# Retention attention by pairs of units, grouped by the tiling of TensorE

## The chip, the cores and the metric

One core of a Trainium2 chip runs the whole program. The metric is the device time in microseconds. Engines: TensorE (PE) multiplies, VectorE (DVE), ScalarE (ACT) and GpSimd (POOL) do the rest, SyncE (SP) issues all DMAs on one queue.

## The reference, cut to what matters

```python
def _attn_ref(q, k, v):                       # B=4, H=8, S=576, D=64
    scores = (1/sqrt(D)) * q @ k.T
    gamma = 1 - 2.0 ** (-5 - arange(H))
    Dmat = where(i >= j, gamma_h ** (i - j), 0)
    return (scores * Dmat) @ v
def _moe_ref(x, w_in, g_ln, w_sg, b_sg, w_out):
    h = gelu(x @ w_in); u, v = h[..., :512], h[..., 512:]
    v_n = (v - mean) / sqrt(var + 1e-6) * g_ln
    v_s = einsum('ts,bsd->btd', w_sg, v_n) + b_sg[None, :, None]
    return x + (u * v_s) @ w_out
def _moe2_ref(x, g_ln, w_ch1, w_ch2):
    return x + relu(layernorm(x) * g_ln @ w_ch1) @ w_ch2
out = _moe2_ref(_moe_ref(_attn_ref(q, k, v)))
```

## The kernel before

The program is written out in order by hand: each engine executes its instructions in the order of the code, and nothing is moved later. PSUM has 8 banks in a ring; one of them, `b_75`, belongs to the decoding of weights.

**Attention.** A unit n is one batch and one pair of heads: 16 units, 128 partitions for two heads of 64. A sequence is four chunks of 128 positions and a rest of 64. The decay of the reference is split into a factor of the row (i), a factor of the column (j) and a state carried from chunk to chunk. For a unit: `load_unit` fetches q, k, v (1120 KB in one DMA, five buffers); `prep_unit` scales k on ACT; `scores` (L246) multiplies q and k, and a mask is applied as PSUM is read (L256; on DVE, each fourth on ACT and POOL); `states` (L282) sums k times v by chunk and a scan (L290, DVE) carries them on; `attend_near` (L315) adds masked scores times v, `attend` (L327, L346) the carried state times q. `scores` of the rest (L269) and `attend_rest` (L303) run once in two units. DVE multiplies the result by the factors of the rows and writes it to `xb` (L333, L350). PE is used in tiles here: 64x128 (L246), 64x64 (L303, L327, L346, L269) and 128x64 (L282, L315). The masks (`form_masks`, L499; `form_rest`, L507) are formed from a table during the warm-up products (L530), the rows by four products with K=8 (`form_rows`, L515).

**Gated MLP.** For each batch b: v tiles (`v_tile`, 5 or 4), u chunks (`u_chunk`, 4), spatial gate (`sg_chunk` L706, 4), `w_out_tile`. Each float32 operand is a high and a low part and each product three products (`mm3`, L137 to L139). The low part of the normalized v (`vnl`, L645) and of weights (`split`, L361) is subtracted on POOL. In `sg_chunk` DVE multiplies the gate into u (L724, L727), ACT casts the high part `glh` (L735), and POOL or DVE subtracts `gll` (L738).

**Third part.** In the last batch, the features of `moe2` are scaled (L939), mixed on POOL (L953) and split (`split_features`, L960 on ACT and L961 on DVE).

**The decoding of weights.** w_in, w_out and w_ch come as words of float64. A piece is four steps on DVE (L156, L160, L163, L165) with one square on ACT (L162); after it the weight is split, or stored by DMA. `w_sg` is float32 and only split (ACT L360, L394, and POOL). `background(n)` does the next n steps. How many steps stand where is written in two tables: `UNIT`, two digits for each unit of attention, and `PACE`, for each b the digits of v tiles, u chunks, sg chunks and w_out tiles. What is left is drained after the u chunks of b=3, ahead of `split_features`:

```python
        if last:
            for _ in bg:
                pass
            free(f64_at[2])
...
            feat = split_features(0)
            next(feat)
```

Of the kernel before, what the change touches and what calls it, by code (L numbers as in the profile page):

```python
# [21 lines left out]
NP = H // 2  # L22
# [21 lines left out]
    ("13446", "3140", "2211", "01021"),  # L44
# [3 lines left out]
UNIT = "00 00 21 22 31 11 10 12 21 13 22 11 32 20 01 32".split()  # L48
# [26 lines left out]
O_MASKR = 16  # L75
O_HEAD = O_MASKR + NP * R
O_GROW = O_HEAD + C
TA = O_GROW + NP * C
TS = (NP + 1) * C
# [8 lines left out]
def const_tables():  # L88
    g = np.array(GAMMA, np.float64)
    p = np.arange(128)  # L90
    tab = np.zeros((128, TF + TS), np.float64)
    tab[:, O_TRI:O_TRI + C] = np.arange(C)[None, :] >= p[:, None]
    tab[:, O_GP:O_GP + H] = g[None, :] ** -p[:, None]
    tab[:, O_GK:O_GK + H] = g[None, :] ** (C - p[:, None])
    for hp in range(NP):
        gp = g[2 * hp + p // D][:, None]
        tab[:, O_GC + hp * NC:O_GC + (hp + 1) * NC] = gp ** C * (np.arange(NC)[None, :] > 0)
        tab[:, O_GR + hp:O_GR + hp + 1] = gp ** -(p % R)[:, None]
        tab[0:H, TF + (hp + 1) * C:TF + (hp + 2) * C] = np.arange(H)[:, None] == 2 * hp + p[None, :] // D
    tab[0:H, TF:TF + C] = g[:, None] ** np.arange(C)[None, :] / np.sqrt(D)  # L100
    return tab.astype(np.float32)
# [3 lines left out]
def kernel(  # L105
# [7 lines left out]
    tab_in: bass.AP,  # L113
    params: bass.AP,
# [74 lines left out]
    ld = es_a.enter_context(tc.tile_pool(name="ld", bufs=5))  # L189
# [8 lines left out]
    first = pa.tile([128, D * NC], F32, tag="y", bufs=3, name="first")  # L198

    def load_tab(part):  # L200
        if part == 0:
            nc.sync.dma_start(out=first[:, 0:TF], in_=tab_in[:, 0:TF])
        else:
            nc.sync.dma_start(out=tab[0:H, O_HEAD:], in_=tab_in[0:H, TF:])

    NU = B * NP
    units = {}
# [3 lines left out]
    def load_unit(n):  # L211
        t = ld.tile([128, AW], F32, tag="ld", name="ld")
        if n == 0:

            to, src = (z[:, 0:2 * S].rearrange("p (a s) -> p a s", a=2) for z in (t, attn[n]))
            for x, y in ((0, 2 * C), (2 * C, S)):
                nc.sync.dma_start(out=to[:, :, x:y], in_=src[:, :, x:y])
                if x == 0:
                    load_tab(0)
            nc.sync.dma_start(out=t[:, 2 * S:], in_=attn[n, :, 2 * S:])  # L220
        else:
            nc.sync.dma_start(out=t, in_=attn[n])
        units[n] = dict(ld=t)

    def prep_unit(n):
        u = units[n]
        hp = n % NP
        t = u["ld"]
        u["qT"] = t[:, 0:S]
        u["kT"] = t[:, S:2 * S]  # L230
        u["k"] = t[:, 2 * S:2 * S + NC * C].rearrange("p (c e) -> p c e", c=NC)
        o = 2 * S + NC * C
        v = t[:, o:]
        u["v"] = v
        for h in range(2):
            k = u["k"][:, :, h * D:(h + 1) * D]
            act.activation(out=k, in_=k, func=ACTF.Copy, scale=col(tab, 2 * hp + h))

    def scores(n):
        u = units[n]  # L240
        hp = n % NP
        p = u["p"] = pa.tile([128, 2, NC, C], F32, tag="p", name="p")
        sc = [bank() for h in range(2)]
        for c in range(NC):
            for h in range(2):
                pe.matmul(  # L246
                    sc[h][:, c * C:(c + 1) * C], u["kT"][h * D:(h + 1) * D, c * C:(c + 1) * C],
                    u["qT"][h * D:(h + 1) * D, c * C:(c + 1) * C], start=True, stop=True,
                )
        for h in range(2):  # L250
            x = sc[h].rearrange("p (c i) -> p c i", c=NC)
            on = dve
            if h and n % 2:
                act.copy(p[:, h], x)
                x, on = p[:, h], pool
            on.tensor_tensor(  # L256
                out=p[:, h], in0=x, in1=mask[:, 2 * hp + h].unsqueeze(1).to_broadcast([128, NC, C]), op=ALU.mult,
            )
            free(sc[h])
        if n % 2 == 0:  # L260
            return

        rest = u["rest"] = bank()
        pr = u["pr"] = pa.tile([128, 2 * R], F32, tag="pr", name="pr")
        for x in range(2):
            w = units[n - 1 + x]
            for h in range(2):
                r = slice(h * D, (h + 1) * D)
                pe.matmul(  # L269
                    rest[r, x * R:(x + 1) * R], w["kT"][r, NC * C:], w["qT"][r, NC * C:], start=True, stop=True,  # L270
                    skip_group_check=True,
                )
        dve.tensor_tensor(out=pr, in0=rest[:, 0:2 * R], in1=col(tab, O_MASKR + (hp - 1) * R, 2 * R), op=ALU.mult)

    def states(n):
        u = units[n]
        us = bank()
        us_c = us[:, 0:NC * D].rearrange("p (e c) -> p c e", c=NC)
        for c in range(NC):
            for h in range(2):  # L280
                r = slice(h * D, (h + 1) * D)
                pe.matmul(  # L282
                    us_c[r, c], u["k"][:, c, r],
                    u["v"][:, c * C + h * D:c * C + (h + 1) * D], start=True, stop=True,
                )


        y = pa.tile([128, D * NC], F32, tag="y", bufs=3, name="y")
        u["y"] = y.rearrange("p (e c) -> p c e", c=NC)
        dve.tensor_tensor_scan(  # L290
            out=y, data0=decay[:, n % NP], data1=us[:, 0:NC * D], initial=0.0, op0=ALU.mult, op1=ALU.add
        )
        free(us)

    def attend_rest(n):
        if n % 2 == 0:
            return
        u = units[n]
        for x in range(2):
            o = u["rest"][:, (2 + x) * R:(3 + x) * R]  # L300
            for h in range(2):
                r = slice(h * D, (h + 1) * D)
                pe.matmul(  # L303
                    o[r], units[n - 1 + x]["v"][r, NC * C:], u["pr"][r, x * R:(x + 1) * R], start=x == 0, stop=False,
                    skip_group_check=True,
                )

    def attend_near(n):
# [1185 lines left out]
```

## Time and profile before

| what | value |
|---|---|
| median of 3 runs | 662.07 us (661.23 to 662.87) |
| the profiled execution | 661.1 us |
| span in the trace | 659.3 us |
| granted TensorE clock, mean | 1.000 |
| PE, busy share of the span | 99% |
| DVE, ACT, POOL | 70%, 47%, 46% |

The span runs from the first to the last instruction that the profiler recorded; the execution's own time is 1.8 us longer. All times of the trace are microseconds from the span's start. A timeline row is: start, duration, engine, line, operation, out<-in with shapes, number of instructions joined in the row, and in brackets an idle time ahead of it and what ended it. The durations of joined PE rows overlap, so a rate is read from start to start. Attention runs to 78.4 us, the gated MLP to about 285, and the third part to the end.

### The profile page before, as it was taken

The numbers are of one execution on the slowest core, as the hardware profiler recorded it, in microseconds if no ns is written. First come the engines' busy times: TensorE is split into PE (matmuls) and PEld (weight loads), VectorE is DVE, ScalarE is ACT, GpSimd is POOL, SyncE is SP. The second block draws the span as 40 slices with busy tenths as digits, with TensorE's granted clock in tenths as the row PEclk, the third lists the DMA queues.
The fourth block names the chain that finished last, engine by engine and source line by source line (L and its number), as shares of the span: only waits on it lengthen the run. The fifth ranks groups of instructions, "written<-read, shape, count | busy, mean of one in ns | idle before, by whom it ended". The sixth has DMA issues, their size and how long they took to land.

```text
span 659.3 us, 12482 instructions
## 1 busy us (share of the span) xinstructions
PE 652.3 (99%) x4428; PEld 592.9 (90%) x4428; DVE 458.7 (70%) x925; ACT 310.7 (47%) x638; POOL 306.0 (46%) x290
## 2 busy tenths in 40 slices
PE   8999999999999999999999999999999999999997
PEld 6888899899889989998898889988898889999996
DVE  5799769789799885877888643555543345458894
ACT  4454595275277457524454533233535313335443
POOL 0354658225325617955555694265558742410000
PEclk9999999999999999999999999999999999999999
DMA  8999638677687685579996868799999689999734
GB/s 317 365 371 352 192 106 231 228 243 231 225 296 230 194 244 135 173 276 398 310 309 245 266 209 269 241 369 371 341 354 373 200 299 342 363 364 413 263 129 160
DMA packets 97230, 181.23 MB, mean 275 GB/s; under 512 B 9608, under 2 KB 47112, under 8 KB 93456
## 3 DMA queue, kind: packets, MB, share of 16 engines
q1 hardware_dynamic: 97168, 180.44, 80.7%
q8 instruction: 35, 0.57, 0.3%
q14 instruction: 27, 0.22, 0.1%
HBM read 122.99 MB, written 56.62 MB: 272 GB/s over the span
## 4 chain that ended last, share of the span: by engine, by line
PE 92%; DVE 3%; DMA 2%; ACT 2%; POOL 1%; issue 1%; SPq 0%; DVEq 0%; POOLq 0%; ACTq 0%
PE b L139 24%; PE b L137 23%; PE b L138 23%; PE b L788 6%; PE b L1265 3%; PE b L246 2%; PE b L315 2%; PE b L327 2%; PE b L1266 2%; DMA raw<-in_w_in_dram 1%; PE b L282 1%; PE b L530 1%; PE b L722 1%; PE b L721 1%; POOL vnl L645 1%
## 5 line engine op out<-in xcount | busy, mean ns | idle before, releaser
L137 PE MATMUL b<-fe,w 128*128 128x384 f32 x336 | 113.2, 337 | 0.0
L139 PE MATMUL b<-fe,w 128*128 128x384 f32 x336 | 113.0, 336 | 0.0
L138 PE MATMUL b<-fe,w 128*128 128x384 f32 x336 | 112.7, 335 | 0.0
L139 PE MATMUL b<-w,h 128*128 128x512 f32 (+1 forms) x270 | 98.1, 363 | 0.0
L138 PE MATMUL b<-w,h 128*128 128x512 f32 (+1 forms) x270 | 97.9, 363 | 0.0
L137 PE MATMUL b<-w,h 128*128 128x512 f32 (+1 forms) x270 | 96.8, 358 | 0.0
L869 POOL TENSOR_TENSOR w<-raw_w,w 128x512 fp32r<-128x512 f32 x30 | 39.6, 1321 | 58.3 <-ACT w L868 53.2
L137 PEld LDWEIGHTS b<-fe,w 128*128 128x128 f32 x336 | 63.1, 188 | 3.8 <-DVE t L1122 0.9
L138 PEld LDWEIGHTS b<-fe,w 128*128 128x128 f32 x336 | 63.1, 188 | 2.7
L139 PEld LDWEIGHTS b<-fe,w 128*128 128x128 f32 x336 | 63.0, 188 | 0.0
L139 PEld LDWEIGHTS b<-w,h 128*128 128x128 f32 x270 | 51.0, 189 | 7.7
L137 PEld LDWEIGHTS b<-w,h 128*128 128x128 f32 x270 | 51.0, 189 | 6.0 <-issue 0.2
L138 PEld LDWEIGHTS b<-w,h 128*128 128x128 f32 x270 | 50.9, 189 | 6.1
L162 ACT ACTIVATE raw<-raw 128x512 f32<-128x512 f32 x44 | 29.9, 679 | 54.5 <-DVE b L160 47.3
L1099 ACT ACTIVATE h<-b 128x384 fp32r<-128x384 f32 x32 | 15.7, 491 | 82.7 <-DVE b L1128 54.7
L589 POOL TENSOR_TENSOR st<-st,par 128x1 f32<-128x1 f32 x36 | 22.1, 616 | 49.6 <-DVE st L588 49.5
L1100 DVE SCALAR_TENSOR_TENSOR h<-b,h 128x384 fp32r<-128x384 f32 x32 | 17.8, 556 | 30.7 <-ACT h L1099 30.7
L137 PE MATMUL b<-w_sg,vnh 128*128 128x288 f32 x128 | 37.8, 295 | 0.0
L139 PE MATMUL b<-xt_hi,w_in 128*128 128x288 f32 x128 | 37.7, 295 | 0.0
L139 PE MATMUL b<-w_sg,vnl 128*128 128x288 f32 x128 | 37.7, 295 | 0.0
L138 PE MATMUL b<-w_sg,vnh 128*128 128x288 f32 x128 | 37.7, 295 | 0.0
L138 PE MATMUL b<-xt_lo,w_in 128*128 128x288 f32 x128 | 37.7, 294 | 0.0
(196 smaller groups left out, 1695.3 us busy)
## 6 DMA issues: line engine op xcount, KB each, us to landing
w<-ws_dram SPq DMA_DIRECT2D x96, 256.0 KB, 5.0
ld<-in_attn_dram SPq DMA_DIRECT2D x15, 1120.0 KB, 8.4
raw<-in_w_ch_dram SPq DMA_DIRECT2D x32, 512.0 KB, 4.9
ws_dram<-w SPq DMA_DIRECT2D x16, 896.0 KB, 7.6
w<-wb_dram SPq DMA_DIRECT2D x14, 1024.0 KB, 7.9
w_dram<-c SPq DMA_DIRECT2D x32, 256.0 KB, 3.1
wb_dram<-fe SPq DMA_DIRECT2D x32, 256.0 KB, 5.1
raw_w<-w_dram SPq DMA_DIRECT2D x30, 256.0 KB, 4.3
```

Of the source, the lines that this page charges most:

```text
L137: pe.matmul(ps, lh, rh, start=first, stop=False, skip_group_check=True)
L138: pe.matmul(ps, lh, rl, start=False, stop=False, skip_group_check=True)
L139: pe.matmul(ps, ll, rh, start=False, stop=last, skip_group_check=True)
L162: act.activation(out=f(w1), in_=f(w1), func=ACTF.Square)
L246: pe.matmul(sc[h][:, c * C:(c + 1) * C], u["kT"][h * D:(h + 1) * D, c * C:(c + 1) * C], u["qT"][h * D:(h + 1) * D, c * C:(c + 1) * C], sta ...
L315: pe.matmul(o[r, c * C:(c + 1) * C], v[:, c * C + h * D:c * C + (h + 1) * D], p[:, h, c], start=(c == 0), stop=(c == NC - 1), skip_group_c ...
L589: pool.tensor_tensor(out=st[:, 4:5], in0=st[:, 3:4], in1=col(par, O_MH), op=ALU.pow)
L788: pe.matmul(ps, g, wo[k][:, w], start=done[0] == 1, stop=done[0] == 3 * KE, skip_group_check=True)
L869: pool.tensor_tensor(out=t[:, 1], in0=raw, in1=f(t[:, 0]), op=ALU.subtract)
L1099: act.activation(out=t[:, 0], in_=v, func=ACTF.Relu)
L1100: dve.scalar_tensor_tensor(out=t[:, 1], in0=v, scalar=0.0, in1=f(t[:, 0]), op0=ALU.max, op1=ALU.subtract)
L1265: pe.matmul(ps, e[:, 0, x], t, start=begin, stop=False, skip_group_check=True)
```

## The change

- Units go in pairs (a, b). The products of a pair stand in three groups by PE's tiling: scores of both (64x128); rest scores, the far part and the rest of the pair before (64x64); states and near part (128x64). The far part of a pair thus comes one pair later (`finish(k - 1)`).
- The factors of the rows are multiplied into q on POOL (`scale_q`) and no longer into the result; ACT copies the result to `xb` (`put`). All masks are on DVE.
- The loads are split in two: `kk` (544 KB, four buffers) and `qv` (576 KB, six buffers).
- The rows are formed by two products of 128x128 by 512 columns after the first scores; the masks are formed from their PSUM banks by DVE (L537, L546) after that, in place of the warm-up.
- `v_products(0, 0)` of the gated MLP, which ran inside the last unit, stands behind attention.
- Attention has 32 background steps, in `PAIR`, where there were 44. In b=3 the v tiles have none, and the u chunks twelve; w_in is decoded with its right half first. `w_sg` is cast in b=0.

PE, one pair of units ahead of it and behind it in the same pattern: before (a row of `L246` stands for alternating rows of two banks; `b_..` are PSUM banks, `ld` a unit's load, `p` and `pr` masked scores, `y` the carried states):

```order
L246 MATMUL b_79<-ld 128x128
...
L303 MATMUL b_78<-pr,ld 64x64 x4
L282 MATMUL b_76<-ld 64x64 x8
L315 MATMUL b_77<-p,ld 64x128 x8
L327 MATMUL b_77<-ld,y 64x128 x6
L346 MATMUL b_78<-ld,y 64x64 x4
L246 MATMUL b_80<-ld 128x128
...
L269 MATMUL b_80<-ld 64x64 x4
L282 MATMUL b_82<-ld 64x64 x8
L315 MATMUL b_76<-p,ld 64x128 x8
L327 MATMUL b_76<-ld,y 64x128 x6
```

and now (`kk` and `qv` are the two loads):

```order
L254 MATMUL b_81<-qv,kk 128x128
L254 MATMUL b_76<-qv,kk 128x128
...
L273 MATMUL b_81<-qv,kk 64x64 x4
L325 MATMUL b_82<-qv,y 64x128 x6
L325 MATMUL b_78<-qv,y 64x128 x6
L340 MATMUL b_80<-pr,qv 64x64 x4
L340 MATMUL b_80<-qv,y 64x64 x4
L294 MATMUL b_76<-qv,kk 64x64 x16
L316 MATMUL b_79<-p,qv 64x128 x8
L316 MATMUL b_77<-p,qv 64x128 x8
```

The tiling changes eight times in two units before, and three times now.

ACT behind attention, in the v tiles of b=0 (`t` is a v tile after GELU, `vnh` the high part of its normalized form), before:

```order
L619 ACT_TABLE_LOAD
L619 ACTIVATE t,st<-b_79 128x512
L619 ACTIVATE t,st<-b_82 128x512
L603 ACTIVATE st<-st 128x1
L604 ACTIVATE vnh,st<-t,st 128x512
L360 CAST w_out<-c 128x512
L162 ACTIVATE raw<-raw 128x512
```

and now:

```order
L658 ACT_TABLE_LOAD
L658 ACTIVATE t,st<-b_81 128x512
L658 ACTIVATE t,st<-b_78 128x512
L642 ACTIVATE st<-st 128x1
L643 ACTIVATE vnh,st<-t,st 128x512
L362 CAST w_in<-c 128x512
L362 CAST w_sg<-raw_sg 128x576 x2
L658 ACTIVATE t,st<-b_79 128x512
L642 ACTIVATE st<-st 128x1
L643 ACTIVATE vnh,st<-t,st 128x512
L362 CAST w_sg<-raw_sg 128x576 x2
L396 CAST w_sg<-raw_sg 128x576
```

The five casts of `w_sg` moved here out of attention, and w_out's went behind them.

DVE from the u chunks of b=3 to the first sg multiply (`x_t` is a turned tile of x, `fe` a feature part), before:

```order
L759 STREAM_TRANSPOSE x_t<-xb 128x4x4x32 x3
L961 TENSOR_TENSOR fe<-x_raw,fe 128x768
L759 STREAM_TRANSPOSE x_t<-xb 128x4x2x32
L724 SCALAR_TENSOR_TENSOR b_78<-b_78,par,b_bc 128x288
L727 TENSOR_TENSOR u<-u,b_78 128x288
```

and now, where the rows of `L154` to `L163` stand once before these, and once more ahead of the last piece:

```order
L154 TENSOR_SCALAR b_75<-raw 128x512
L158 SCALAR_TENSOR_TENSOR b_75<-raw,b_75 128x512
L161 SCALAR_TENSOR_TENSOR b_75<-raw,b_75 128x512
L163 SCALAR_TENSOR_TENSOR c<-raw,b_75 128x512
L798 STREAM_TRANSPOSE x_t<-xb 128x4x4x32 x2
...
L1000 TENSOR_TENSOR fe<-x_raw,fe 128x768
L798 STREAM_TRANSPOSE x_t<-xb 128x4x2x32
L763 SCALAR_TENSOR_TENSOR b_76<-b_76,par,b_bc 128x288
L766 TENSOR_TENSOR u<-u,b_76 128x288
```

Five pieces of four steps, three in the u chunks and two drained, now stand on DVE between the last v tile's normalization and `L1000`; before there was none.

The diff, cut to its core:

```diff
-    ("13446", "3140", "2211", "01021"),
+    ("00000", "4440", "2211", "01021"),
...
-UNIT = "00 00 21 22 31 11 10 12 21 13 22 11 32 20 01 32".split()
+PAIR = "01 12 12 22 22 22 23 34".split()
...
+    def load_kk(n):
+        if n < NU:
+            t = kk[n] = ld.tile([128, S + NC * C], F32, tag="kk", bufs=4, name="kk")
+            for x, y in ((0, S + NC * C),) if n else ((0, S), (S, S + NC * C)):
+                nc.sync.dma_start(out=t[:, x:y], in_=attn[n, :, x:y])
+                yield
...
+    def scale_q(n):
+        q = units[n]["qT"]
+        row = col(tab, O_LATE + n % NP * C, C)
+        x = q[:, 0:NC * C].rearrange("p (c i) -> p c i", c=NC)
+        pool.tensor_tensor(out=x, in0=x, in1=row.unsqueeze(1).to_broadcast([128, NC, C]), op=ALU.mult)
+        x = q[:, NC * C:]
+        pool.tensor_tensor(out=x, in0=x, in1=row[:, 0:R], op=ALU.mult)
...
+    def put(n):
+        u = units[n]
+        b, hp = divmod(n, NP)
...
+        act.copy(xb[b][:, hp, 0:NC * C], u["o"])
+        free(u["o"])
...
-        for k in range(KE):
-            t = slot("w_in").rearrange("p (a n) -> p a n", a=2)
-            wi.append(t)
-            for x in range(0, F1, 512):
+            wi.append(slot("w_in").rearrange("p (a n) -> p a n", a=2))
+        for x in (512, 0):
+            for k in range(KE):
...
+    def form_rows():
+        for x in range(2):
+            pe.matmul(each[x], one, grow[:, x * 512:(x + 1) * 512], start=True, stop=True)
...
+    def form_masks(x):
+        for h in range(x * 4, x * 4 + 4):
+            dve.scalar_tensor_tensor(
+                out=mask[:, h], in0=each[x][:, h % 4 * C:(h % 4 + 1) * C], scalar=col(first, O_GP + h),
+                in1=col(first, O_TRI, C), op0=ALU.mult, op1=ALU.mult,
+            )
...
+    def finish(k):
+        for n in (2 * k, 2 * k + 1):
+            far(n)
+            put(n)
+        attend_rest(k)
+        put_rest(k)
+
+    for k in range(NPAIR):
+        a, b = 2 * k, 2 * k + 1
+        scores(a)
+        if k == 0:
+            form_rows()
+            scale_k(a)
+            form_masks(0)
+        masks(a)
+        if k == 0:
+            form_decay()
+            form_late()
+            free(each[0])
+            states(a)
+            form_rest()
+        else:
+            scale_k(a)
+        if k == 1:
+            finish(k - 1)
+            load(load_qv(a + 4), load_qv(b + 4))
+        scores(b)
+        masks(b)
+        scale_k(b)
+        scores_rest(k)
+        mask_rest(k)
+        scale_q(a)
+        scale_q(b)
+        background(1 if k == 0 else int(PAIR[k][0]))
+        if k == 0:
+            form_masks(1)
+            free(each[1])
+        if k > 1:
+            finish(k - 1)
+            load(load_qv(a + 4), load_qv(b + 4))
+        if k:
+            states(a)
+        states(b)
+        scans(k)
+        near(a)
+        near(b)
+        load(load_kk(a + 4), load_kk(b + 4))
+        background(int(PAIR[k][1]))
...
+    finish(NPAIR - 1)
     es_a.close()
...
-            v_tile(0, 0, v_ps)
+            v_tile(0, 0)
```

## Rows read from the trace of the kernel before

**Rows 1.** The page: busy time of each engine, its share and instructions.

```profile
PE 652.3 (99%) x4428; PEld 592.9 (90%) x4428; DVE 458.7 (70%) x925; ACT 310.7 (47%) x638; POOL 306.0 (46%) x290
```

**Rows 2.** What PE waited for: engine, line, releaser: us in total, times, longest.

```profile
PE b L530 <- ACT zero L495: 2.3, 1, 2.3
PE b L315 <- POOL p L256: 0.2, 1, 0.2
```

**Rows 3.** Timeline of PE over one pair of units in attention's middle.

```profile
43.82 1.16 PE L246 MATMUL b<-ld 64*128 64x128 f32 x16
44.91 0.45 PE L269 MATMUL b<-ld 64*64 64x64 f32 x8
45.29 0.69 PE L282 MATMUL b<-ld 128*64 128x64 f32 x16
45.81 1.05 PE L315 MATMUL b<-p,ld 128*64 128x128 f32 x16
46.78 0.98 PE L327 MATMUL b<-ld,y 64*64 64x128 f32 x12
...
52.00 0.38 PE L246 MATMUL b<-ld 64*128 64x128 f32 x2
```

**Rows 4.** Timelines of PE and of DVE at the start.

```profile
8.44 1.15 PE L515 MATMUL b<-tab 8*128 8x128 f32 x8
3.82 1.66 DVE L499 TENSOR_SCALAR formed<-first 128x128 f32<-128x128 f32 x8 [2.42 <-DMA first<-in_tab_dram]
5.40 2.12 DVE L507 TENSOR_SCALAR tab<-first 64x64 f32<-64x64 f32 x8
8.54 1.29 DVE L256 TENSOR_TENSOR p<-b,formed 128x512 f32<-128x512 f32 x2 [1.02 <-PE b L246]
20.64 0.69 DVE L156 TENSOR_SCALAR b<-raw 128x512 uint32<-128x512 uint32 x1
```

**Rows 5.** Busy time in windows of 5 us; the last columns are PE's clock, DMA share, GB/s.

```profile
35.00:40.00 5.00, 5.00 (x88) 4.42 (x86) 5.00 (x11) 2.25 (x6) 1.48 (x2) 1.00 1.00 397
45.00:50.00 5.00, 5.00 (x98) 4.45 (x100) 4.93 (x10) 3.45 (x7) 3.51 (x3) 1.00 0.88 315
```

**Rows 6.** b=0: timelines of PE, ACT, POOL; PE's chain; DMA issues to 80 us.

```profile
78.45 0.50 PE L137 MATMUL b<-w_in,xt_hi 128*128 128x512 f32 x1
79.21 1.28 ACT L619 ACT_TABLE_LOAD   x1
101.43 0.62 ACT L644 CAST vnh<-t 128x512 fp32r<-128x512 f32 x1
102.72 1.31 POOL L645 TENSOR_TENSOR vnl<-t,vnh 128x512 fp32r<-128x512 f32 x1
104.08 0.40 PE b L722
raw_sg<-in_w_sg_dram SPq DMA_DIRECT2D x5, 288.0 KB, 3.2
```

**Rows 7.** b=3: timelines of DVE, ACT and PE.

```profile
242.57 0.69 DVE L156 TENSOR_SCALAR b<-raw 128x512 uint32<-128x512 uint32 x1
245.42 0.15 DVE L588 TENSOR_SCALAR st<-st 128x1 f32<-128x1 f32 x1
258.44 1.92 DVE L961 TENSOR_TENSOR fe<-x_raw,fe 128x768 fp32r<-128x768 f32 x1 [3.52 <-ACT fe L960]
260.64 0.48 DVE L724 SCALAR_TENSOR_TENSOR b<-b,par,b_bc 128x288 f32<-128x288 f32 x1
262.46 2.22 DVE L961 TENSOR_TENSOR fe<-x_raw,fe 128x768 fp32r<-128x768 f32 x1
269.68 0.95 DVE L961 TENSOR_TENSOR fe<-rows,fe 128x768 fp32r<-128x768 f32 x1
269.80 0.62 ACT L735 CAST glh<-u 128x512 fp32r<-128x512 f32 x1 [1.73 <-DVE u L727]
271.24 2.91 PE L788 MATMUL b<-w_out,glh 128*128 128x512 f32 x12
```

More of the change, by code (lines that the diff above doesn't have):

```diff
@@ L209 @@
     xt = {}
[L211 to L223, printed above, removed]
@@ new lines, in masks, with scores_rest @@
+    def masks(n):
+        u = units[n]
+        p = u["p"] = pa.tile([128, 2, NC, C], F32, tag="p", name="p")
+        for h in range(2):
+            dve.tensor_tensor(
+                out=p[:, h], in0=u["sc"][h].rearrange("p (c i) -> p c i", c=NC),
+                in1=mask[:, 2 * (n % NP) + h].unsqueeze(1).to_broadcast([128, NC, C]), op=ALU.mult,
+            )
+            free(u["sc"][h])
+    rests = {}
+    def scores_rest(k):
+        t = rests[k] = bank()
+        for x in range(2):
+            u = units[2 * k + x]
+            for r in half:
+                pe.matmul(
+                    t[r, x * R:(x + 1) * R], u["kT"][r, NC * C:], u["qT"][r, NC * C:], start=True, stop=True,
+                    skip_group_check=True,
+                )
@@ L244, in scores, with mask_rest, states @@
+    def mask_rest(k):
+        pr = units[2 * k]["pr"] = pa.tile([128, 2 * R], F32, tag="pr", name="pr")
+        dve.tensor_tensor(
+            out=pr, in0=rests[k][:, 0:2 * R], in1=col(tab, O_MASKR + 2 * k % NP * R, 2 * R), op=ALU.mult
+        )
+    sums = {}
+    def states(n):
+        k, x = divmod(n, 2)
+        if x == 0:
+            sums[k] = bank()
+        u = units[n]
+        o = sums[k][:, x * NC * D:(x + 1) * NC * D].rearrange("p (e c) -> p c e", c=NC)
         for c in range(NC):
@@ L260, in scores @@
[L260 to L292, printed above, removed]
-        free(us)
@@ L295, in attend_rest @@
[L295 to L308, printed above, removed]
+                    o[half[h], c], u["k"][:, c, half[h]], u["v"][:, c * C + h * D:c * C + (h + 1) * D],
@@ new lines, in states, with scans @@
+                    start=True, stop=True, skip_group_check=True,
+                )
+    def scans(k):
+        us = sums.pop(k)
+        for x in range(2):
+            y = pa.tile([128, D * NC], F32, tag="y", bufs=4, name="y")
+            units[2 * k + x]["y"] = y.rearrange("p (e c) -> p c e", c=NC)
+            dve.tensor_tensor_scan(
+                out=y, data0=decay[:, (2 * k + x) % NP], data1=us[:, x * NC * D:(x + 1) * NC * D], initial=0.0,
+                op0=ALU.mult, op1=ALU.add,
+            )
+        free(us)
@@ L309, in attend_near, with near @@
+    def near(n):
         u = units[n]
@@ L522 @@
-    act.copy(col(tab, 0, H), col(first, O_GK, H))
-    for hp in range(NP):
-        act.copy(
-            decay[:, hp].rearrange("p (e c) -> p e c", c=NC),
-            col(first, O_GC + hp * NC, NC).unsqueeze(1).to_broadcast([128, D, NC]),
-        )
-    warm = bank()
-    for _ in range(WARM):
-        pe.matmul(warm, zero[:, 0:128], zero, start=True, stop=True)
-    free(warm)
-    for hp in range(NP):
-        form_masks(hp)
-    form_rest()
-    prep_unit(0)
-    scores(0)
-    form_rows()
```

237 lines of the change are left out of this document (112 added, 125 removed).

## The prediction, made before the run

> **What bounds the kernel now.** I read the page first. TensorE is busy in 99% of the span, and no other engine in more than 70% [rows 1]; the list of what PE waited for holds two waits, 2.3 us for the first memset and 0.2 us in unit 1 [rows 2]. So only two things can move the time: PE work that goes away or is added, and a wait that PE gets where it has none. The timeline of PE over one pair of units then prices the work [rows 3], the timelines of the first 10 us price the start [rows 4], and those of b=0 and b=3 show how late DVE, ACT and POOL may be before PE waits [rows 6, 7]. All sums are made against the profiled execution, 661.1 us, which lies 0.97 us under the median of 662.07; I add that at the end. A measurement of this kernel can tell about 0.3%, or 2.0 us.
>
> **Attention: the switches of tiling.** Busy PE hides a cost between groups of different tile sizes. From start to start, L246 takes 1.09 (43.82 to 44.91) and L315 0.97 (45.81 to 46.78), each for 16 products of 128 columns; L246 has another tiling ahead of it and behind it, L315 only behind [rows 3]. If a switch's price s is shared by the two sides, the 0.12 is half of it: s = 0.24. The second pair has products of 64 columns: L269, eight, between two switches, takes 0.38 (44.91 to 45.29), and L282, sixteen, with one switch ahead of it, 0.52 (45.29 to 45.81). With x for eight products, x + s = 0.38 and 2x + s/2 = 0.52 give x = 0.22 and s = 0.16. I take 0.17, near the second pair, since there the switch is half of what is measured and in the first a tenth. A pair of units has 8 switches now, and 3 in the new order (64x128, then 64x64, then 128x64; first order excerpt): 5 fewer, 0.87 us a pair and 6.9 for eight; with the last unit's own switches 7.2. With the ends of attention left as they are, bounds are 5.2 at 0.13 and 9.6 at 0.24.
>
> **Attention: what is added.** The rows are formed by two products of 512 columns in place of four of 128. The L515 group takes 1.15 with the tail of its last product and a switch in it [rows 4], so 512 columns cost about 0.9; twice that in place of once is +0.9. The larger addition is at the start. DVE formed masks from 3.82, under the warm-up, eight of L499 at 0.2 and eight of L507 at 0.265 [rows 4]. Now L537 reads PSUM, so nothing is formed before the row products end, which is near 9.6 for the first (8.44 + 0.9 and the way to DVE). Ahead of near(1) DVE then has four L537 (0.9), two masks of unit 0 (1.2 by L256), form_rest (2.1 as L507) and two masks of unit 1 (1.2): 9.6 + 5.4 = 15.0 [rows 4]. PE comes to near(1) earlier. I put its waits at 2.6: 0.4 for states(1) behind ACT's scaling, 0.8 for near(1), 0.9 for a bank of pair 1's scores, whose masks stand on DVE behind the first L154, which waits for its raw weight until about 20 us (20.64 before [rows 4]), and 0.5 for pair 2's far part. Bounds: 1.0 if only the first two hold, and 4.5 if the bank's wait comes in two pairs more. In a later pair DVE has four masks, rest mask, two scans and about one decode piece, 2.4 + 0.3 + 1.2 + 2.5 = 6.4 us of a new period of 7.3: enough. ACT's put and POOL's scale_q are off PE's path by a period.
>
> The sum for attention is -7.2 + 0.9 + 2.6 = **-3.7**; its end moves from 75.5 (the first product behind it at 78.45 [rows 6], less the 2.9 of v product (0,0) that ran inside it, twelve products of 512 columns like the L788 row [rows 7]) to 71.8.
>
> **The loads.** Each unit's 1120 KB come as 544 and 576 KB. At a pair period of 7.3 us, two units and one 512 KB weight piece are 2.8 MB, 385 GB/s. The window from 35 to 40 us gives 397 GB/s, and that from 45 to 50, with its engines 88% busy, 315 [rows 5], so it is just enough. The first of these has 512 KB weight pieces among the 1120 KB loads and was full all the same, so I charge the smaller loads nothing and keep the poor window as a rival. The Trainium skill ("DMA: Bandwidth & Descriptors", the table of measured bandwidth) speaks against the split: it asks for at least 1 MiB in a transfer for three quarters of the peak. By it the halves would run slower, and the sum would be that of rival 3; by the row it stays.
>
> **b=0: most of the gain is not handed on.** Attention now has 32 background steps in place of 44; w_sg's five pieces are cast by ACT in b=0's v tiles (second order excerpt). Before, ACT runs from the table load at 79.21 to the last cast of vnh, 101.43 + 0.62 = 102.05; POOL then needs vnl, 102.72 + 1.31 = 104.03, and PE's L722 starts at 104.08 [rows 6], with no slack at all. Afterwards the table load waits for v product (0,0), 71.8 + 2.9 = 74.7. ACT's work up to the last cast is about the same (five w_sg casts in place of three w_out casts and three squares), but the third and fourth w_sg casts want raw buffers that come free only after POOL's subtraction (1.31, as vnl) and a load (3.2): 4.5 less some 2 us of other ACT work leaves 2.6 of waiting [rows 6]. So the last cast ends at 74.7 + 22.84 + 2.6 = 100.1, and POOL's w_out subtraction and vnl bring L722 to about 102.5. PE would be there at 104.08 - 3.7 = 100.4: it waits 2.1, and **-1.5** is handed on. Bounds: 0 (the casts wait once more) and -3.7 (ACT has room in other places).
>
> **b=3: a new wait.** The three pieces not decoded in attention push all later ones back; b=3 keeps five, three in its u chunks and two drained behind them (third order excerpt). A piece takes DVE 242.57 to 245.42, 2.85 us [rows 7], about 2.95 with its neighbours. All five stand on DVE ahead of the feature split L1000 and of the first sg multiply. Before, DVE had 3.5 us of idle time there, and L961 started at 258.44 only because ACT's fe was late; the first multiply was at 260.64 [rows 7]. Now DVE starts the first piece when the last normalization is through, near 247.4; five pieces are 14.75, four turns of x 2.6, the st group 0.75, and 1.6 is lost where a square on ACT stands behind GELU and the scaling of features: 267.0 for L1000 and 268.1 for the first multiply, 7.5 later. From there DVE makes up about 1 us, since L1000 runs beside an idle POOL (0.95 as at 269.68, not 1.92 or 2.22 [rows 7]). ACT's cast of glh for m=2 starts not at 269.80 but at 276.3 and ends at 276.9. PE's w_out tile starts at 271.24 and needs it four products later, 271.24 + 4 x 0.23 = 272.15 [rows 7]. PE waits **4.7 us**; bounds 3.0 (two more us made up) and 6.5 (the square waits twice). No wait would come if the first multiply were at 262.4 or earlier. PE has no idle time behind it in which this could be made up [rows 2].
>
> **The sum.** -1.5 + 4.7 = +3.2: 664.3 against 661.1, and 665.3 against the median; I round to **665.0**.
>
> **The rivals.**
> 1. *DVE's queue in b=3 is short enough* (chance 0.27). For it: DVE's 3.5 us idle there, and ACT starts earlier because v tiles of b=3 lose five squares (its five decode pieces). Against it: 14.75 us of decode does not fit between 247.4 and 262.4 beside 3.3 of turns and st. If it fits up to 1 us, the time is 662.07 - 1.5 to -3.7 + 0 to 1, 658.4 to 661.5: faster.
> 2. *The wait and the full gain* (0.15): ACT in b=0 keeps up, -3.7 + 4.7 = +1.0, or -3.7 + 3 = -0.7: 661.4 to 663.1, no change that could be told.
> 3. *The loads decide attention* (0.08). At 315 GB/s [rows 5] 2.8 MB take 8.9 us, no less than the old period of 8.18 (43.82 to 52.00, [rows 3]); it decides from a period of 7.3, 385 GB/s. Attention then gains nothing, so b=0 hands on nothing: 662.07 + 4.7 = 666.8, up to 670.
> 4. *A switch costs nothing* (0.03): the difference between L246 and L315 is then the tile, and only +0.9, +2.6 and +4.7 are left, about 669.
>
> **How the numbers follow.** The forecast itself has 0.47, and its own range by the bounds is 662.6 to 667.5. Below 660.1 lies rival 1 with most of its chance: faster 0.24. Within 2.0 us of 662.07 lie the rest of rival 1, rival 2 and the low end of the forecast: 0.23. Slower 0.53. The range 658.8 to 667.8 takes in the forecast and all but the best end of rival 1, and leaves out the loads and the costless switch.
>
> **What would show it.** Right: pairs of about 7.3 us on PE; the first v product behind attention near 71.8; a wait of PE for POOL's vnl of some 2 us at sg chunk 0 of b=0; in b=3 five pieces back to back on DVE, the first L763 near 266.6 (268.1 less the 1.5), and a wait of PE of 4 to 5 us at the first w_out tile for glh. Wrong: no wait at that tile; a wait of PE for a load in the pairs; a period of 8 us; an end of attention near 75.

## The result and the profile after

| | before | after |
|---|---|---|
| median | 662.47 us (661.23 to 664.12, 4 runs) | 672.29 us (669.72 to 673.35, 4 runs) |
| ratio of after to before | | 1.0141 [1.0104, 1.0178] |
| profiled execution, its span | 661.1, 659.3 us | 669.72, 667.8 us |
| mean granted clock | 1.000 | 0.995 |

The change makes the kernel slower by 1.4%, where 665.0 was forecast: attention became 1.9 us shorter, and two later stages became 11.0 longer. The profiled execution is the quickest of the four; the other three had clocks of 0.986 to 0.992.

Line numbers have moved: far part L325, near part L316, w_out tile L827, sg multiply L763 and L766, glh L774, gll L777, vnl L684. The page, to be held against [rows 1]:

```profile
PE 650.6 (97%) x4424; PEld 593.2 (89%) x4424; DVE 454.5 (68%) x912; ACT 317.6 (48%) x657; POOL 319.4 (48%) x314
PEclk9999998999999999899999999999999999999999
```

PE's busy time fell by 1.7 us and the span rose by 8.5. What PE waited for stood in two rows [rows 2]; now:

```profile
PE b L827 <- ACT glh L774: 3.5, 2, 2.0
PE b L511 <- ACT zero L507: 2.3, 1, 2.3
PE b L316 <- DVE p L260: 2.1, 2, 2.0
PE b L761 <- POOL vnl L684: 1.5, 1, 1.5
PE b L137 <- POOL vnl L684: 0.8, 1, 0.8
PE b L273 <- DVE p L260: 0.8, 3, 0.4
PE b L254 <- DMA qv<-in_attn_dram: 0.7, 1, 0.7
PE b L827 <- POOL gll L777: 0.6, 1, 0.6
PE b L294 <- DVE p L260: 0.2, 1, 0.2
```

Without the first memset the new waits add up to 10.2: 3.8 in attention, 2.3 ahead of b=0's sg chunks, 4.1 at b=3's first w_out tile. From the first product of each stage to that of the next:

| stage | before | after | difference |
|---|---|---|---|
| attention (before: 78.45 less the v product inside, 2.9) | 75.55 | 73.64 | -1.9 |
| v tiles and u chunks of b=0 | 26.63 | 26.43 | -0.2 |
| sg chunks of b=0 | 15.14 | 19.64 | +4.5 |
| from behind b=0's sg chunks to w_out of b=3 | 153.92 | 153.88 | 0.0 |
| w_out of b=3 to the first hidden product | 13.63 | 20.17 | +6.5 |
| third part | 374.43 | 374.04 | -0.4 |
| span | 659.3 | 667.8 | +8.5 |

**Attention.** The timeline of PE over a pair of units, to be held against [rows 3], has a period of 7.41 (33.87 to 41.28) in place of 8.18:

```profile
33.87 2.06 PE L254 MATMUL b<-qv,kk 64*128 64x128 f32 x32
35.88 0.45 PE L273 MATMUL b<-qv,kk 64*64 64x64 f32 x8
36.16 1.66 PE L325 MATMUL b<-qv,y 64*64 64x128 f32 x24
...
38.45 1.15 PE L294 MATMUL b<-qv,kk 128*64 128x64 f32 x32
39.43 1.92 PE L316 MATMUL b<-p,qv 128*64 128x128 f32 x32
41.28 0.94 PE L254 MATMUL b<-qv,kk 64*128 64x128 f32 x12
```

Eight pairs give 6.2, the first scores come 0.55 earlier, the row products cost 0.8, and the waits 3.8: -2.1, against -1.9 measured. The 0.55 is no gain of the change: with the same start, the first scores come at 6.64 in e4 and at 7.70 in e16 below, whose four warm-up products take 3.62 where those of the changed kernel take 2.72. Counted from its first scores on, attention takes 66.9 for 68.2 before. At the start, the timelines of PE, DVE and POOL:

```profile
16.29 0.43 PE L316 MATMUL b<-p,qv 128*64 128x128 f32 x2 [1.95 <-DVE p L260]
11.29 1.16 DVE L546 SCALAR_TENSOR_TENSOR tab<-tab,first 64x64 f32<-64x64 f32 x1
13.09 1.23 DVE L546 SCALAR_TENSOR_TENSOR tab<-tab,first 64x64 f32<-64x64 f32 x1
11.10 1.27 POOL L241 TENSOR_TENSOR qv<-qv,tab 128x512 f32<-128x512 f32 x1 [10.66 <-ACT tab L530]
12.95 1.28 POOL L241 TENSOR_TENSOR qv<-qv,tab 128x512 f32<-128x512 f32 x1
```

`form_rest` (eight L546) takes 4.2 where L507 took 2.1 [rows 4]. Six of the eight take 0.28 to 0.31; these two, beside `scale_q` on POOL, end 0.1 behind POOL's instruction. The masks of unit 1 stand behind them, and PE waits 1.95.

**b=0.** The timelines of ACT and PE, and the windows; before, see [rows 6]:

```profile
76.74 1.28 ACT L658 ACT_TABLE_LOAD   x1 [1.63 <-PE b L137]
87.65 0.68 ACT L362 CAST w_sg<-raw_sg 128x576 fp32r<-128x576 f32 x1 [2.88 <-DMA raw_sg<-in_w_sg_dram]
102.48 0.61 ACT L683 CAST vnh<-t 128x512 fp32r<-128x512 f32 x1
102.60 0.40 PE L137 MATMUL b<-w_sg,vnl 128*128 128x288 f32 x1 [0.83 <-POOL vnl L684]
105.07 0.61 PE L761 MATMUL b<-w_sg,vnl 128*128 128x288 f32 x1 [1.54 <-POOL vnl L684]
105.48 0.44 PE L135 MATMUL b<-w_sg,vnh 128*128 128x288 f32 x1
105.72 0.44 PE L136 MATMUL b<-w_sg,vnh 128*128 128x288 f32 x1
106.00:108.00 2.00, 2.00 (x10) 2.00 (x10) 1.97 (x5) 1.75 (x4) 1.91 (x3) 0.50 0.68 183
```

The last cast of vnh ends at 103.09, 26.35 behind the table load. Behind the two waits the products come 0.24 apart (105.48 to 105.72) in place of 0.13, until 108.1, and the granted clock is 0.50, its 1.2 GHz level. The waits are 2.4 (0.83 and 1.54), and the stage is 4.5 longer.

**b=3.** The timelines of DVE, ACT, POOL and PE; before, see [rows 7]. Windows of 5 us follow:

```profile
258.01 0.69 DVE L163 SCALAR_TENSOR_TENSOR c<-raw,b 128x512 f32<-128x512 f32 x1 [1.82 <-ACT raw L160]
270.40 0.49 DVE L763 SCALAR_TENSOR_TENSOR b<-b,par,b_bc 128x288 f32<-128x288 f32 x1
277.78 0.62 ACT L774 CAST glh<-u 128x512 fp32r<-128x512 f32 x1 [1.22 <-DVE u L766]
276.31 0.73 POOL L867 TENSOR_TENSOR x_raw<-raw_w 128x256 f32<-128x256 f32 x1 [1.70 <-DMA raw_w<-w_dram]
273.59 0.63 PE L827 MATMUL b<-w_out,glh 128*128 128x512 f32 x2
275.73 0.73 PE L827 MATMUL b<-w_out,glh 128*128 128x512 f32 x2 [1.51 <-ACT glh L774]
278.45 3.43 PE L827 MATMUL b<-w_out,glh 128*128 128x512 f32 x8 [1.99 <-ACT glh L774]
283.19 1.19 PE L827 MATMUL b<-w_out,gll 128*128 128x512 f32 x4 [0.60 <-POOL gll L777]
```

```profile
275.00:280.00 5.00, 2.28 (x7) 1.52 (x8) 4.90 (x10) 2.26 (x5) 3.61 (x4) 0.89 0.98 354
280.00:285.00 5.00, 4.40 (x15) 3.15 (x14) 3.16 (x4) 4.46 (x7) 5.00 (x7) 0.77 0.12 46
```

The waits are 4.1 and the stage is 6.5 longer: many of the products behind them run at the lower clock again, eight in 3.4 us.

### The profile page after: what moved, and what is told of

It is laid out like the page before. It is cut to its first block, busy times and chain, and to the rows that moved or that the text cites. A ratio compares the mean times of both kernels' runs of the same rounds, so it can differ in the third digit from the quotient of the medians.

```text
span 667.8 us, 12565 instructions
## 1 busy us (share of the span) xinstructions
PE 650.6 (97%) x4424; PEld 593.2 (89%) x4424; DVE 454.5 (68%) x912; ACT 317.6 (48%) x657; POOL 319.4 (48%) x314
## 4 chain that ended last, share of the span: by engine, by line
PE 78%; DVE 7%; ACT 5%; DMA 3%; issue 3%; POOL 3%; SPq 1%; DVEq 0%; ACTq 0%; POOLq 0%
PE b L137 21%; PE b L136 21%; PE b L135 20%; PE b L827 6%; PE b L1304 3%; DMA raw<-in_w_in_dram 2%; PE b L1305 2%; PE b L254 1%; PE b L325 1%; PE b L316 1%; DVE b L158 1%; ACT t L655 1%; DVE c L163 1%; PE b L294 1%; POOL vnl L684 1%
## 5 line engine op out<-in xcount | busy, mean ns | idle before, releaser
L827 PE MATMUL b<-w_out,glh 128*128 128x512 f32 x128 | 38.1, 403 | 3.5 <-ACT glh L774 3.5
```

Source lines behind the costliest of these rows:

```text
L827: pe.matmul(ps, g, wo[k][:, w], start=done[0] == 1, stop=done[0] == 3 * KE, skip_group_check=True)
```

## The experiments

The theory after the result: the change's schedule of decoding makes two waits, and behind each TensorE runs some products at 1.2 GHz. The rivals: the new attention itself costs time, or the lower clock has its own cause. In the table "sg" is b=0's sg chunks and "out" b=3's stage from w_out to the first hidden product (15.14 and 13.63 before, 19.64 and 20.17 after).

| run | median us | ratio to before | what stood out |
|---|---|---|---|
| e1_fill | 674.99 | 1.0187 [1.0154, 1.0220] | sg 18.39, out 24.56 |
| e2_b3_early | 678.16 | 1.0243 [1.0199, 1.0287] | b=3's sg chunks 25.28, out 13.64 |
| e3_before_sched | 673.48 | 1.0174 [1.0136, 1.0211] | sg 21.22, out 20.65 |
| e4_rest_late | 672.56 | 1.0141 [1.0099, 1.0182] | attention to 74.05 |
| e5_sg_early | 676.44 | 1.0203 [1.0179, 1.0227] | sg 15.29, attention to 84.11 |
| e6_late8 | 671.92 | 1.0145 [1.0120, 1.0171] | out 13.63, third part 8.5 longer |
| e7_both | 677.09 | 1.0212 [1.0188, 1.0235] | attention to 82.19 |
| e8_start | 678.99 | 1.0218 [1.0187, 1.0250] | attention to 82.31 |
| e9_mix_late | 671.63 | 1.0143 [1.0120, 1.0166] | out 19.34 |
| e10_sg_raw | 668.59 | 1.0101 [1.0076, 1.0126] | sg 15.51, out 21.83 |
| e11_sg_pace | 671.24 | 1.0137 [1.0116, 1.0158] | out 13.63, sg chunks of b=2, b=3 19.68, 20.95 |
| e12_all | 673.01 | 1.0160 [1.0132, 1.0189] | first scores at 9.14 |
| e13_mix_fill | 672.69 | 1.0181 [1.0148, 1.0214] | out 17.70, 3.86 of it dummies |
| e14_sg_pace2 | 668.62 | 1.0104 [1.0086, 1.0123] | out 21.00, waiting for gll |
| e15_start | 668.52 | 1.0102 [1.0082, 1.0121] | attention to 75.14 |
| e16_raw_w | 663.20 | 1.0014 [0.9997, 1.0030] | out 15.45 |
| e17_all | 662.84 | 1.0003 [0.9987, 1.0020] | attention to 74.61 |
| e18_start_fill | 662.65 | 1.0008 [0.9994, 1.0023] | clock stays up at the start |

**Schedule or attention: e3.** The kernel before, its attention untouched, with the change's order of w_in and its tables (in `UNIT` 32 steps spread over the units):

```diff
-    ("13446", "3140", "2211", "01021"),
+    ("00000", "4440", "2211", "01021"),
...
-UNIT = "00 00 21 22 31 11 10 12 21 13 22 11 32 20 01 32".split()
+UNIT = "00 00 21 21 20 11 10 11 11 12 21 11 21 10 01 21".split()
```

> The kernel before, its attention untouched, with the change's decode schedule: 32 steps in attention (UNIT 00 00 21 21 20 11 10 11 11 12 21 11 21 10 01 21), w_in's right halves first, PACE[3] of the change. Theory A (the schedule alone makes the loss): w_sg is cast in b=0 and PE waits 2 to 3 us for vnl in its first sg chunk, waits about 4 us for glh at b=3's first w_out tile, and both times the clock falls; 662.5 + 4 + 6 = 672, within 3 us. Rival D (the pairs make the loss, by engines that are late behind the new attention): 662 to 665 and no such waits.

It has nearly the waits of the changed kernel (glh 3.9 for 3.5, vnl 1.5 and 0.8 as there) and its time. So the schedule alone makes the loss. The new attention hardly gains: by the same count as above, e3's attention, in the old order, takes 67.4 from its first scores on, the changed kernel's 66.9, and that of the runs which leave it as changed (e1, e2, e6, e9 to e11, e13, e14, e16) 66.2 to 68.9. The new attention with the old schedule was not run.

**The clock: e1, e9, e13.** e1 puts dummy products, whose result is overwritten, where PE waits:

```diff
+            if b == 0 and m == 0 and x == 0:
+                for _ in range(25):
+                    pe.matmul(o, wsl[0][0][:, 0:128], wsl[0][0][:, 0:HALF], start=True, stop=True)
...
+        if b == B - 1 and i == 0 and done[0] == 0:
+            for _ in range(17):
+                pe.matmul(ps, wo[0][:, 0, 0:128], wo[0][:, 0], start=True, stop=True, skip_group_check=True)
```

> The changed kernel with dummy products where PE waits: 25 of 288 columns ahead of the first sg half of b=0, 17 of 512 columns ahead of the first w_out tile of b=3. They take about as long as PE's waits there (2.4 and 4.1 us), so the waits for vnl, glh and gll stay where they are in time, but PE is busy through them. Theory A (PE's idling costs twice, once as the wait and once as a stretch at the half clock behind it): the granted clock is 1.000 throughout, and the time falls by about 3.3 us, 1.2 at b=0 and 2.0 at b=3, to 669 where the changed kernel has 672.3. Rival B (the half clock has another cause, the load of all engines together for instance, and comes anyway): the clock still falls behind 104 and 279 us, and the time is the same or some tenths longer.

In b=0 the 25 products add 3.3, 0.9 more than the 2.4 of waits that they replace, and yet the sg chunks take 1.25 less than after the change: the waits had cost 2.1 beyond their own length. The window that had 0.50 is now:

```profile
106.00:108.00 2.00, 2.00 (x15) 1.78 (x14) 1.83 (x3) 1.47 (x3) 2.00 (x2) 1.00 0.96 293
```

In b=3 the dummies only moved the wait: PE then waited 4.1 for gll, which POOL subtracts behind a mix (L867) that waits for `raw_w`. So e9 put both `mix_w1(0, *)` behind the last sg chunk:

> The changed kernel with the two mixings of w1 on POOL (L867 to L871), which stood between the gll subtractions of b=3's sg chunks, moved behind the last sg chunk. Theory P (POOL's gll for m=2 ends b=3's loss: POOL waits for raw_w until 276 and mixes ahead of it, so gll for m=2 comes 3 us after its glh): from the first w_out tile to the first hidden product 17 to 18 us, not 20.2, the time falls by 2 to 3 us, and the stretch at the half clock stays. Rival Q (glh and the half clock behind it set the end, POOL's gll is hidden by them): 20 us as before.

The wait for gll is gone and that for glh stays at 3.5; the stage is 0.8 shorter only, with the clock still low (0.90 and 0.76 from 275 to 285). e13 is e9 with e1's 17 products, and its windows follow:

> e9_mix_late with 17 dummy products of 512 columns ahead of the first w_out tile of b=3, as in e1_fill. POOL's gll is early here, so the wait for glh is what is left. Theory A (the idling of PE costs a second time, by the half clock behind it): no fall of the clock at b=3, and from the first w_out tile to the first hidden product 13.6 + 3.9 of dummies = 17.5 us, and less than 0.5 of waits, where e9_mix_late had 19.3 us; the time falls by 1.8 us against it, to 669.8. Rival B: 19 us or more, and a fall of the clock or a wait in another place.

```profile
275.00:280.00 5.00, 5.00 (x22) 3.87 (x22) 4.90 (x10) 2.27 (x5) 3.04 (x4) 1.00 0.98 371
280.00:285.00 5.00, 5.00 (x23) 4.13 (x22) 3.29 (x5) 1.50 (x3) 3.56 (x6) 1.00 0.12 43
```

The clock stays at 1.00, and with 3.9 of dummies the stage takes 1.6 less than in e9 with 3.5 of waits. So 2.0 is what the waits of e9 cost there beyond their own length. The whole does not profit: the third part, with 3.2 of waits for DVE's u and t, is 1.8 longer than e9's, and the median is 672.69 where 669.8 was expected.

**The raw buffers of w_sg: e10.** Four of the five loads go into free u tiles, all five at the first step:

```diff
-            for x in range(2) if k < 0 else (k + 2,) if k + 2 <= NC else ():
-                ahead.append(rawp.tile([128, 1024], F32, tag="raw", name="raw_sg")[:, 0:S])
-                nc.sync.dma_start(out=ahead[x], in_=w_sg[x])
+        for x in range(NC + 1):
+            if x < NC:
+                t = t1.tile([128, 2, HALF], F32, tag="u", bufs=4, name="raw_sg").rearrange("p x n -> p (x n)")
...
+            nc.sync.dma_start(out=t, in_=w_sg[x])
```

> The changed kernel with w_sg's five raw tiles in five buffers (four of the u tiles, which are free then, and one of the raw tiles), all loaded at the first step of w_sg in the v tiles of b=0. Theory A (the two casts that wait for a raw buffer, 3.2 us of ACT's idle time, make the wait for vnl at the first sg chunk): no idle of ACT ahead of a cast, PE's wait there below 0.3 us, the four sg chunks of b=0 take 15 us, not 19.6, and the time falls by 4.5 us to 667.5. Rival F (ACT's load as such): PE still waits over 1.5 us.

No cast waits, PE's wait for vnl is 0.4, and b=0's sg chunks take 15.51: 4.1 of the 4.5 are gone. The ratio falls by 0.0040, 2.6 us, since attention ended 2.0 later (its first scores came 0.9 later, and the clock was 0.82 and 0.84 from 15 to 25) and b=3 took 1.7 more.

**Other places for the decoding: e2, e5, e6, e11 and combinations.** e2 decodes in b=3's v tiles (`"34440", "4100"`), e5 casts w_sg inside attention, behind four pieces of w_in, e6 leaves three more pieces to the third part (`LATE` 8, `PACE[4]` `"1222"`, b=3's row as before), e11 is e10 with eight more steps in the w_out tiles of b=0 and b=1 and the three pieces that are then left in b=3's v tiles.

> The changed kernel with PACE[3] at 34440 for the v tiles and 4100 for the u chunks: the same pieces, but decoded beside b=3's v tiles and in its first u chunk; nothing is left to drain. Theory A (DVE's queue of five pieces ahead of the sg multiplies makes all of b=3's loss): no wait of PE at the first w_out tile, no fall of the clock there, first sg multiply about 262 to 263, and the time falls by 6.1 us, to about 666. Rival C (the loss at b=3 comes from something else that is late in the new order, so that DVE's queue hides it): a wait for glh of over 2 us stays, and the time falls by less than 3 us.

> The changed kernel with another order of the background: w_sg is cast and split after the first four pieces of w_in, inside attention, and two of w_in's left halves are decoded in b=0's v tiles in its place. The number of steps in attention stays 32. Theory A (ACT's chain in b=0, held up by w_sg's raw buffers, makes PE wait for vnl, and the half clock behind it costs as much again as half the wait): the idle times of ACT in the v tiles go, PE waits less than 0.5 us at the first sg chunk, that chunk's four take 15 us in place of 19.6, and the time falls by 4 to 5 us, to 668. Rival F (ACT's load as such is too much, not its waiting): PE still waits 1.5 us or more, and the time falls by less than 2 us.

> The changed kernel with three more pieces of w_ch decoded in the third part (LATE 8, PACE[4] 1222) and the old row of PACE for b=3, so that b=3 keeps two pieces, in its v tiles, as the kernel before had them. Theory A (five pieces on DVE ahead of the sg multiplies make b=3's loss): from the first w_out tile of b=3 to the first hidden product 13.6 us as before, not 20.2; the time falls by 6.5 us, to 666, unless DVE in the third part becomes late. Rival C (another engine or a transfer is late there in the new order): a wait of over 2 us stays at that tile.

> e10_sg_raw with eight more decode steps in the w_out tiles of b=0 (53333) and b=1 (35530), where DVE idles 3 us each, and b=3's last twelve in its v tiles (1344, none in the u chunks), so that DVE is free ahead of the sg multiplies as in the kernel before. Theory A: the first w_out tile of b=3 to the first hidden product takes 13.6 us, no fall of the clock, and only attention's gain is left: 672.3 - 4.6 - 6.5 = 661. Rival: the decode steps delay x_r or v tiles in b=1 or b=2 and PE waits there for 2 us or more.

Each removes the wait that it aims at and makes another. In e2 and e11 the store of a decoded piece (`w_dram<-c`) lands late, and the next L163 waits 5.9 and 5.7 for its buffer; vnh and vnl stand behind. In e5 ACT's put to `xb` stands behind the casts (PE waits 3.6 for it). In e6 the third part waits 4.2 for DVE's t. e7 (e5 and e6), e8 (e7 with the start in another order) and e12 (e11 with e9 and the row products first, which then took 2.89 us in place of 1.98) brought no more than these (677.09, 678.99, 673.01).

**DVE's order at the start: e4, e15, e18.** e4 moves `form_rest()` behind `masks(b)`; e15, on top of e14 below, forms the rows before the first scores and moves the second half of the masks and `form_rest` behind the scan, and the first decode step one pair later.

> The changed kernel with form_rest (eight L546 on DVE, 4.2 us there) moved from ahead of unit 1's masks to behind them. Theory E (DVE's forming of the rest masks ahead of masks(1) makes the 2 us wait of near(1)): that wait falls below 0.5 us, attention ends 1 to 2 us earlier, near 72. By theory A most of it is not handed on, since ACT's chain in b=0 decides: 672.3 - 1, PE waiting up to 1 us more at the sg chunk of b=0. Rival: pair 1 then waits for the scans or for mask_rest(0) just as long, and attention ends at 73.6 as before.

> e14_sg_pace2 with the row products ahead of the first scores (three warm-up products stay), and in pair 0 masks of both units, scans, the second half of the masks and the rest masks in this order, the first decode step one pair later. Theory E: PE's waits for masks in the first 30 us fall from 2.5 to 3 us to about 1, attention ends 1 to 2 us earlier, and the time falls by as much against e14_sg_pace2. Rival: DVE's work up to 24 us is the bound in any order, the waits move to pr or to pair 1's masks, and the end of attention moves by less than 0.7 us.

In both the wait only changes its name: 2.1 for the scan's y in e4, 1.8 for the rest mask pr in e15. So it looks as if DVE's work up to 24 us is the bound in either order. e18, on top of e16 below, fills the wait with two products of 512 columns:

> e16 with two dummy products of 128x128 by 512 columns (0.95 each, as the row products) in front of the near part of unit 1, where PE waits 2 us for DVE's masks; their result is overwritten. In e16 the granted clock falls to 0.85 and 0.81 from 15 to 25 us, behind that wait. If the idle time is what lowers the clock: 1.00 in both windows, and attention from its first scores to the first v product, 68.9 in e16, 1.3 to 1.7 shorter; the time some 661.5, which can't be told from the kernel before. If the clock falls for another reason: windows as in e16, and 68.9 or up to 2 more.

The windows of e16, where nothing fills it, then of e18:

```profile
15.00:20.00 5.00, 2.86 (x29) 2.04 (x27) 4.89 (x14) 0.00 (x0) 0.69 (x2) 0.85 1.02 398
20.00:25.00 5.00, 5.00 (x72) 4.66 (x70) 2.29 (x4) 2.06 (x5) 1.28 (x1) 0.81 0.79 305
```

```profile
15.00:20.00 5.00, 4.83 (x43) 2.83 (x41) 4.89 (x14) 0.00 (x0) 0.09 (x1) 1.00 1.02 407
20.00:25.00 5.00, 4.76 (x96) 4.39 (x97) 3.08 (x6) 2.24 (x5) 2.48 (x3) 1.00 0.98 360
```

The clock stays up, and attention takes 67.74 from its first scores on in place of 68.93. That this is the clock's doing is not shown: e16 waits 1.2 for loads there and e18 does not, and e14, unfilled, with windows of 0.83 and no wait for a load, takes 67.87. The time is not to be told from e16's; b=2's sg chunks took 1.4 more.

**The second chain of b=3: e14, e16, e17.** e14 is e10 with pieces taken forward, none left to drain:

```diff
-    ("00000", "4440", "2211", "01021"),
+    ("13400", "4440", "2211", "01021"),
```

> e10_sg_raw with PACE[3] at 1340 for the v tiles and 4440 for the u chunks: two pieces more ahead of b=3's feature loads, three in the u chunks behind them, none drained. Theory A: no decoded piece is stored while the feature loads fill the queue, so no wait as in e2 and e11; DVE is through with the pieces 5.9 us earlier than in the change, first sg multiply near 264.5, and PE's wait for glh at the first w_out tile falls below 0.5 us; from there to the first hidden product 14 to 15 us. 668.6 - 7 = 661.5, as the kernel before or up to 1.5 us under it. Rival: the wait for a store or for vnl comes again, 666 or more.

The first multiply comes at 265.10 in place of 270.40 and the wait for glh is 0.5, yet the stage takes 21.0. PE now waits 3.8 for gll. POOL and SP in e14:

```profile
272.32 0.73 POOL L871 TENSOR_TENSOR x_raw<-raw_w 128x256 f32<-128x256 f32 x1 [3.01 <-DMA raw_w<-w_dram]
262.05 6.37 SPq L809 DMA_DIRECT2D x_dram<-x_t  x12
268.52 0.37 SPq L865 DMA_DIRECT2D raw_w<-w_dram  x1
```

SP issues twelve stores of the turned x ahead of the load of `raw_w`, and these take it 6.4 us. e16 issues that load behind `u_chunk(3, 2)`, ahead of the stores (its buffer is allocated there, and `load_w1` no longer loads it):

```diff
             u_chunk(b, m)
+            if last and m == 2:
+                first_w1 = rawp.tile([128, 1024], F32, tag="raw", name="raw_w1")
+                nc.sync.dma_start(out=first_w1, in_=w1_dram[0])
             turn_x(b, m)
```

> Gate weights in buffers of their own, two of the drained pieces of b=3 taken forward (e14), and the first raw weight of the third part (raw_w) loaded right behind the u chunks, ahead of the twelve stores of turned x. Theory (the loss of b=3 is a chain on two queues: DVE's pieces for glh, and SP's stores ahead of raw_w's load for POOL's mixes and gll): POOL mixes as soon as it is free, near 266.5, the wait for gll (3.8) goes, first w_out tile to first hidden product about 14.2 in place of 21.0, its clock stays up, and the time is about 662. Rival (POOL's mixes are late for their own length, not for the load): the wait for gll stays above 2 us, 20 us or more from the first w_out tile on, 668 to 669.

> e16 with e15's start (rows before the first scores, DVE's order in pair 0). Theory that DVE's work up to 24 us is the bound in any order: as e15 against e14, 0 to 0.5 less than e16, about 661.5 to 662, no difference that can be told from the kernel before. Rival: with b=3 repaired the start's gain shows, about 660.

POOL, SP and a window of e16:

```profile
270.87 0.74 POOL L874 TENSOR_TENSOR x_raw<-raw_w 128x256 f32<-128x256 f32 x1
263.46 0.38 SPq L1032 DMA_DIRECT2D raw_w<-w_dram  x1
280.00:285.00 5.00, 5.00 (x24) 4.13 (x23) 5.00 (x5) 2.71 (x5) 4.84 (x5) 1.00 0.35 105
```

The mix no longer waits, the wait for gll is 0.5, the clock is 1.00 (0.77 and 0.55 from 275 to 285 in e14), the stage takes 15.45, and the time falls by 5.4 us. So e10, e14 and e16 together take the loss back, to 1.0014 of the kernel before; with e15's start 1.0003. No version beat the kernel before.

## Why the prediction was right in its direction and wrong in its size

**Right.** The direction; the period of a pair (7.41 for 7.3); the row products (+0.8 for +0.9); the wait for the late vnl in b=0 (2.4 for 2.1); and DVE's queue in b=3: this stage begins 2.35 later than before, and less that the first multiply is at 268.05 (forecast 268.1) and glh for m=2 is ready at 276.05 (forecast 276.9).

**Attention, "-3.7": it was -1.9.** Two terms were mis-sized. The switches gave 6.2 for 7.2, or 0.15 each for 0.17 if all of the shorter period is theirs. The waits of 2.6 were 3.8: 2.1 for 0.8 ahead of near(1), and 0.7 for a load that had no term, less smaller ones elsewhere. For the first, form_rest was put at "2.1 as L507", though L546 reads two tensors of SBUF and L507 one, and [rows 7] already showed L961 at 0.95, 1.92 and 2.22. The reading of those rows was wrong too: POOL was not idle beside the one of 0.95. It ran L742, which began 0.04 behind L961 and itself took 1.09 where it takes 0.32 at 265.78; the other two began while POOL was at L953. (In the change POOL was idle there, and L1000 took 0.95 as forecast.)

**b=0, "only -1.5 is handed on": it was +2.35, the largest miss, 3.9 us.** The step was right in kind: ACT's chain from the table load to vnl ends last. But it starts where attention ends, so all of attention's shortfall went through it (table load at 76.74 for 74.7), and its waits for raw_sg were 3.2 for 2.6: L761, L722 before, came at 105.07 for 102.5, 2.6 of the 3.9. The step also ended with PE's wait. Eleven products 0.24 apart in place of 0.13 came behind it, 1.2 of the other 1.3. e10 shows the first part and e1 the second.

**b=3, "PE waits 4.7": the waits were 4.1, the loss 6.5.** The wait was counted and what follows it was not: the 2.4 between 4.1 and 6.5, of which e13 against e9 shows 2.0. The text also followed DVE and ACT, and not POOL's gll behind `raw_w` on SP's queue. In the changed kernel it showed as 0.6; e1 and e14 show that alone it costs about as much as glh (4.1 and 3.8 of waits), and in e16 0.5 of it is left.

**The sum** was +3.2 and the span rose by 8.5: 3.9 and 1.8 more at the two waits, less 0.4 in the third part. The median rose by more, 9.8, since the profiled execution lies 2.6 under it, and the one before 1.4 under its own.

**The rivals.** 1 and 2 are out: the wait at w_out is there, and b=0 handed on nothing. 3 is out: in the pairs PE waits once for a load, 0.7 at the start, and e16's and e18's first windows above move 398 and 407 GB/s, as much as the 397 of [rows 5], in loads of 544 and 576 KB and pieces of 512. The Trainium skill ("DMA: Bandwidth & Descriptors", the table of measured bandwidth) asks for 1 MiB or more in a transfer for three quarters of the peak; these windows show no loss by it. 4 is out by the period; its terms add up to 670.3, not to 669. The range left out a time above 667.8 because it took in the bounds of each wait and no cost behind one.

## What to carry to other kernels

A wait put on a TensorE that was busy all along can cost more than its length, here 4.5 for 2.4 and 6.5 for 4.1: look at the granted clock of the windows behind it and add the products that run at the lower level. When work is moved off a full stage, follow every queue that it is moved past, the DMA queue and the second operand's engine among them, since the chain that ends last is followed by one almost as late; here three repairs were needed before the time moved back. And a chain that starts where the shortened stage ends inherits every error made on that stage.

## What the runs showed of the hardware

- **The clock falls behind short waits.** Granted 0.50 behind waits of 0.83 and 1.54 us in b=0, 0.77 behind 1.51 and 1.99 in b=3, 0.81 to 0.85 behind 1.98 at the start of e16; in the changed kernel, whose wait there was 1.95, the windows from 10 to 30 showed 1.00. Filled with products, each of the three places stays at 1.00 (e1 in b=0, e13 in b=3, e18 at the start). It is not the same in each run: of nine kernels whose wait at the start was 1.9 to 2.0, the clock fell from 15 to 25 in the six whose first scores came at 7.50 to 7.70 (e1, e2, e5, e10, e14, e16), and stayed at 1.00 in the three with 6.79 to 7.07 (the change, e9, e13). Why is open. That this makes the spread of the medians is likely and was not tried apart.
- **DVE and POOL hold each other up where both read two operands from SBUF.** All eight L546 after the change, in nanoseconds (least, median, most), then a POOL row before and one after the change:

```profile
L546 DVE SCALAR_TENSOR_TENSOR tab<-tab,first x8: 275/286/1230, 11.3 to 15.2; 64x64 f32<-64x64 f32 x8
269.72 1.09 POOL L742 TENSOR_TENSOR grem<-u,grem 128x64 fp32r<-128x64 f32 x1
277.80 1.99 POOL L777 TENSOR_TENSOR gll<-u,glh 128x512 fp32r<-128x512 f32 x1
```

The two long ones are those beside L241 above; in every run with the new start, each one over 0.35 lay beside an instruction of POOL. POOL waits likewise: L742 began just behind L961 of [rows 7] (0.32 at 265.78), and L777 just behind an L1000 at 277.66 (1.29 at 273.04). The Trainium skill ("GPSIMD Engine Reference", Key points) says that POOL and DVE share their interfaces to SBUF and that there is contention with DVE instructions that have two SBUF inputs; the rows agree.
